# The last forward stage of a recurrent attention kernel: scaled O in the key and query space, P scaled by GpSimd, rows stored by SyncE

## The chip, the cores and the metric

The kernel runs on one core of a Trainium2 chip. The metric is the device time of one execution in microseconds (us), lower is better. Three timed runs of the kernel before gave 2970.79, 2971.32 and 2973.85 us; their median is 2971.32. A separate execution was taken with the profiler.

The engines are named as the profile names them: PE is TensorE (matmuls and transposes, with PEld for its weight loads), DVE is VectorE, ACT is ScalarE, POOL is GpSimd, SP is SyncE, which here only issues DMAs (SPq is its queue). DMAs are issued by SP and POOL, and in places by ACT. L939 is line 939 of the kernel before.

## The reference

The kernel computes the forward pass and all gradients of a conditioned transformer block, in bfloat16, for one sequence of 2048 rows of 512 values. Cut to what matters:

```
mod = silu(c) @ w_mod                      # six rows: sa, ca, ga, sb, cb, gb
h = layernorm(x) * (1 + ca) + sa
mem = mem0                                 # 8 memory rows
for s in range(64):                        # segments of 32 rows
    t = concat(mem, h[32 s : 32 s + 32])   # 40 rows
    q, k, v = t Wq, t Wk, t Wv             # 32 heads of 128
    p = softmax(mask(q k^T / sqrt(128)))
    o = (p v) Wo
    mem = o[:8];  out_s = o[8:]
x1 = x + ga * concat(out_s)
h2 = layernorm(x1) * (1 + cb) + sb
y = x1 + gb * ((sigmoid(h2 w_gate) * (h2 w_up)) w_down)
```

The outputs are y and, for a given grad_out, the gradients of x, mem0, Wq, Wk, Wv, Wo, w_gate, w_up, w_down, c and w_mod.

## The kernel before, in words

The program has four large parts that follow each other on one core: the recurrent attention forward (`phase2`, 64 stages, one per segment, up to about 950 us), the MLP forward and backward (`phase3`, 16 tiles of 128 rows, and its weight gradients), the recurrent attention backward, and the attention's weight gradients. All of the attention's intermediate results that the backward needs are kept in DRAM: V^T (`VT`), O^T (`OT`), P (`PS`), O (`OSR`), and the rows of Q and K (`QST`, `KST`).

**A forward stage.** Four heads' rows stand side by side in a 128-partition tile, three heads of 40 rows (120 columns) in a group, 11 groups in all. PE projects K, Q and V (`pass_ps`, L257 and L677), turns K and Q (L883) into the tiles `kT` and `qT` (128 partitions x 1328 columns of bf16 each), computes the scores (L893), and ACT writes their exponentials into one of two buffers ET (L895; stage s uses ET of number s mod 2). PE sums and multiplies by V (L899, L919), DVE takes the reciprocal of the sums (`rden`, L904), and the unnormalized product is evacuated, scaled by `rden`, into `Ost` by DVE (L950) and ACT (L947). PE turns `Ost` (L911, L960) into `OT`, multiplies by Wo (L223, 64 matmuls into `at_ps`), and the sum of two halves goes back to the next stage as its memory rows. `Ost` is one buffer: SP stores it to `OSR` (L1078), and the next stage may write it when that store has landed.

**P in the stages up to 62.** SP turns ET by a DMA into `Pst` (L1048); one stage later POOL scales it by `rden` in place (L1141, 120x1408 elements) and SP stores it to `PS` (L1144).

**The last stage, 63.** It does not turn by DMA. PE turns V (`turn_v`) and P (`turn_p`, L934, into PSUM tiles `pt_ps`), V^T is copied to the space of rows that are free by then, and DVE scales the turned P out of PSUM into `Pst` (L939, `scale_p`, three instructions). `Pst` is one buffer too, so L939 waits until the store of stage 62's P has landed. SP stores V^T (L1077), `Ost` (L1078), `OT` (L1081), later P (L1149) and the rows of K and Q (`late_rows`, L608 and L609). Rows of the attention's output go to the DRAM array `AOA` by `store_rows` (L347) and by `rows_b` (L811, four stores), both through POOL's queue, here as before. In the same stage POOL issues the loads of the three MLP weights (L987, L1050, L1075; 1792 KB each), into the space of Wk and Wv, and the first MLP tile's input is prepared (`first_tile_steps`).

**The first MLP tiles.** `run_pipeline` runs tiles through the steps `s0` to `s6`, deepest step first. `s0` makes the layernorm of a tile from its attention rows, x and grad_out, which `glu_load` loads through SP (L1177, L1179, L1180): DVE at L1255 to L1281, the power on POOL (L1266), the bf16 copy `xh2` on ACT (L1274; of tile 1 on POOL, L1272). `s2` multiplies by w_gate and w_up in four column chunks: for each a `gp` product (L1322) whose sigmoid ACT writes to `sg` (L1323) and an `up` product (L1326) that ACT copies to `u` (helper `evac`, L61; L63 is its DVE form). The products use a ring of five PSUM banks (`psM`). After tile 0's products PE turns w_down (L1231) through two banks (`psT`) and two of the ring, evacuated by ACT and DVE alternately; `s3` uses the result (L1353). `wT_piece` (L1220) turns w_gate and w_up in the groups after steps 2, 3 and 4 of the pipeline, each turned pair evacuated by ACT or DVE by the parity of its number plus k.

**What sets the order.** The stages' instructions keep the order in which the code writes them (`pin`); in the MLP the order of PE and ACT is written down for the first steps and a list scheduler places the rest. The tiles of the MLP (`u`, `sg`, `hh`, `h2`, ...) lie in SBUF space that the attention's pools have left; the framework adds the waits for what last used the space. Every DMA of SP's and ACT's queues raises one of eight semaphores, in turn, and every DMA of POOL's queue one of another eight.

Of the kernel before, what the change touches and what calls it, by code (L numbers as in the profile page):

```python
# [10 lines left out]
ALU = mybir.AluOpType  # L11
# [29 lines left out]
class K:  # L41
# [72 lines left out]
    def phase0(self):  # L114
        nc, tc, cfg, io = self.nc, self.tc, self.cfg, self.io
        const = self.const
        D, DC = cfg.D, cfg.DC
        self.ident = const.tile([128, 128], BF16, name="ident")
        make_identity(nc, self.ident[:])
        self.foldsel = const.tile([128, 32], BF16, name="foldsel")  # L120
        fs2 = const.tile([128, 2, 32], BF16, name="foldsel2")
        for i in range(2):
            nc.vector.tensor_tensor(fs2[:, i, :], self.ident[:, 64 * i:64 * i + 32], self.ident[:, 64 * i + 32:64 * i + 64],
                                    op=ALU.add)
        nc.vector.tensor_tensor(self.foldsel[:], fs2[:, 0, :], fs2[:, 1, :], op=ALU.add)
        self.foldhalf = fs2
        self.later = []
        self.ones = const.tile([128, 128], BF16, name="ones")
        nc.vector.memset(self.ones[:], 1.0)
        L, M = cfg.L, cfg.M  # L130
        mT32 = const.tile([120, 120], F32, name="maskT32")
        nc.gpsimd.memset(mT32[:], 0.0)
        for b in range(3):
            sl = mT32[:, b * L:(b + 1) * L]
            nc.gpsimd.affine_select(out=sl, in_=sl, pattern=[[1, L]], compare_op=ALU.is_ge, fill=NEG,
                                    base=b * L, channel_multiplier=-1)
            nc.gpsimd.memset(mT32[:, b * L:b * L + M], 0.0)
# [195 lines left out]
    def store_rows(self, psp, pool, ft, dram, name, tag, then=None):  # L333

        nc = self.nc
        tb = pool.tile([128, 128], BF16, name=name + "_tb", bufs=1 if name.endswith("_b") else 2)
        nc.vector.tensor_copy(tb[:].rearrange("p (r c) -> p c r", c=self.cfg.DC), ft[:])

        def f():
            tp = psp.tile([128, 128], BF16, name=name + "_tp", tag=tag)  # L340
            nc.tensor.transpose(tp[:], tb[:], self.ident[:])
            rb = pool.tile([128, 128], BF16, name=name + "_rb")
            nc.vector.tensor_copy(rb[:], tp[:])
            if callable(dram):
                dram(rb)
            else:
                nc.gpsimd.dma_start(dram.rearrange("r (c x) -> (r c) x", x=128), rb[:])  # L347
            if then is not None:
                then(rb)

        self.later.append(f)
# [97 lines left out]
    def phase2(self):  # L449
# [15 lines left out]
        with ExitStack() as ctx:  # L465
# [107 lines left out]
            def part3(t, pi):  # L573
                return t[:, pi * PW:min((pi + 1) * PW, G * GW)].rearrange("p (g x) -> p g x", x=GW)
# [233 lines left out]
            def rows_b(rb, b):  # L808

                for i in range(4):  # L810
                    nc.gpsimd.dma_start(self.AOA[4 * b + i + 1, 32:32 + M, :].rearrange("r (c x) -> (r c) x", x=128),  # L811
                                        rb[32 * i:32 * i + 32, :])

            tail = TailRows(self, sb2, psp, psp, 1, "ao", rows_b, (8, 16, 8), ptag="p", bufs=1)
# [35 lines left out]
            for s in range(NS):  # L850
# [55 lines left out]
                def transposes_part(src, pi, w=GW, m=128):  # L906
# [4 lines left out]
                        nc.tensor.transpose(ps[:, j, 0:m], src[0:m, g * w:g * w + GW], self.ident[0:m, 0:m])  # L911
                    return ps[:, 0:n, 0:m], n

                def pv(pi, or_ps=None):
                    or_ps = or_ps or ps_f32("or_ps")
                    n = min(PG, G - pi * PG)
                    for j in range(n):
                        g = pi * PG + j
                        nc.tensor.matmul(or_ps[:, j, :], lhsT=ET[:, g * GW:(g + 1) * GW], rhs=Vst[:, g * GW:(g + 1) * GW],  # L919
                                         start=True, stop=True)  # L920
                    return or_ps
# [12 lines left out]
                        nc.tensor.transpose(ps[:, j, :], ET[:, g * GW:(g + 1) * GW], self.ident[:, :])  # L934
                    turned_p[pi] = ps

                def scale_p(pi):
                    n = min(PG, G - pi * PG)
                    nc.vector.tensor_tensor(Pst[0:120, pi * PG:pi * PG + n, :], turned_p[pi][0:120, 0:n, :],  # L939
                                            rden[:, pi * PG:pi * PG + n].unsqueeze(2).to_broadcast([120, n, 128]), op=ALU.mult)  # L940

                def ost(pi, or_ps, eng):
                    n = min(PG, G - pi * PG)
                    if eng == "act":
                        for j in range(n):
                            g = pi * PG + j
                            nc.scalar.activation(Ost[0:120, g * GW:(g + 1) * GW], or_ps[0:120, j, :], AF.Copy,  # L947
                                                 scale=rden[:, g:g + 1])
                        return
                    nc.vector.tensor_tensor(part3(Ost, pi)[0:120, 0:n, :], or_ps[0:120, 0:n, :],  # L950
                                            rden[:, pi * PG:pi * PG + n].unsqueeze(2).to_broadcast([120, n, 128]), op=ALU.mult)

                def ott_first():
                    ps, n = transposes_part(Ost, 0, m=120)
                    self.evac("dve", part3(OT, 0)[:, 0:n, 0:120], ps)

                def ott_rest():
                    ps = psp.tile([128, 2 * PG, GW], BF16, name="tps", tag="p")
                    for g in range(PG, G):
                        nc.tensor.transpose(ps[:, g - PG, 0:120], Ost[0:120, g * GW:(g + 1) * GW], self.ident[0:120, 0:120])  # L960
                    for pi in (1, 2):
                        n = min(PG, G - pi * PG)
                        self.evac("act", part3(OT, pi)[:, 0:n, 0:120], ps[:, (pi - 1) * PG:(pi - 1) * PG + n, 0:120])
# [110 lines left out]
                if s == NS - 1:  # L1074
                    nc.gpsimd.dma_start(self.w_down, io["B_w_down"].rearrange("(fc p) d -> p fc d", p=128))  # L1075
                    for g0, t, w in ((0, RAs[0]["k"], 8), (8, RAs[0]["q"], G - 8)):
                        nc.sync.dma_start(self.VT[s, :, g0:g0 + w, :], t[:, 0:w * GW].rearrange("p (g x) -> p g x", x=GW))  # L1077
                nc.sync.dma_start(self.OSR[s], gl3(Ost))  # L1078
                at_ps = outproj()
                if s == NS - 1:  # L1080
                    nc.sync.dma_start(self.OT[s], gl3(OT))  # L1081
# [12 lines left out]
                    self.store_rows(psp, sb2, ft, self.AOA[s + 1, 0:32, :], "at", "p")  # L1094
                    self.pop_later()
                    self.pop_later()
                    turn_p(1)
                    self.pop_later()
                    for pi in (2, 0, 1):
                        scale_p(pi)  # L1100
                    break
                evac_turned()
                if s in first_tile[0]:
# [41 lines left out]

                if s < NS - 1:
                    norms.append(norm)
            self.glu_first[0] = self.glu_load(0, nc.sync)
            nc.sync.dma_start(self.PS[NS - 1], Pst[:])  # L1149
            late_rows()  # L1150
            self.pinned = self.pin(i0)

    def glu_tiles(self):
# [29 lines left out]
    def phase3(self):  # L1183
# [9 lines left out]
        with ExitStack() as ctx:  # L1193
# [32 lines left out]
            def wdT_pieces():  # L1226
                for f0 in range(0, FC, 7):
                    for c in range(DC):
# [4 lines left out]
                                  tp[:, 0:7, :].rearrange("p i f -> p (i f)"))  # L1233

            turns = {2: [wT_piece(w_gate, w_gateT, 0, 4, None)],
                     3: [wT_piece(w_gate, w_gateT, 4, 10, 0), wT_piece(w_up, w_upT, 0, 4, 1)],
                     4: [wT_piece(w_up, w_upT, 4, 10, 1)]}

            ins = {}
# [6 lines left out]
            def s0(j):  # L1246
# [21 lines left out]
                xh2 = sbp.tile([128, D], BF16, name="xh2", bufs=5)  # L1268
                xhf = sbp.tile([128, D], F32, name="xhf", tag="f32tmp", bufs=5)
                nc.vector.tensor_scalar(xhf[:], x1[:], mv[:, 0:1], rstd[:, 0:1], op0=ALU.subtract, op1=ALU.mult)  # L1270
                if j == 1:
                    nc.gpsimd.tensor_copy(xh2[:], xhf[:])  # L1272
                else:
                    nc.scalar.activation(xh2[:], xhf[:], AF.Copy)  # L1274
# [1235 lines left out]
```

## Time and profile before

| What | us |
|---|---|
| median of three runs | 2971.32 |
| the profiled execution's own time | 2972.47 |
| its span, first to last instruction | 2970.7 |
| PE busy | 2903.7 (98%) |
| DVE, ACT, POOL busy | 1624.5, 1341.6, 1237.7 |
| last stage's first K projection (L257) | starts at 930.54 |
| tile 0's first product with w_gate (L1322) | starts at 950.89 |
| tile 1's first product with w_gate | starts at 966.99 |

The page gives busy times, the chain of work that ended last, and the costliest groups; the trace also answers for stretches of time: a timeline of each engine (start, duration, engine, line, operation, and in brackets the idle time before it with what ended it), the waits summed by who waited for whom, and busy times with the granted TensorE clock in chosen windows. A DMA's row on SPq is the time in which SP issued it, not the transfer.

### The profile page before, as it was taken

How to read it: one execution, taken by the hardware profiler on the slowest of the kernel's cores; microseconds unless marked ns; L12 is line 12 of the kernel's file. 1: busy time of each engine (PE TensorE's matmuls, PEld its weight loads, DVE VectorE, ACT ScalarE, POOL GpSimd, SP SyncE). 2: the span in 40 equal slices, each digit the busy share in tenths (PEclk: the TensorE clock that was granted, in tenths of full speed). 3: DMA queues.
4: the chain of work that ended last, by engine and by line, in shares of the span. 5: the costliest groups of instructions: out<-in, count | busy, mean ns of one | idle time of the engine just before them, and what ended most of it. 6: DMA issues, size and time to landing. Idle time of an engine off the chain costs nothing.

```text
span 2970.7 us, 105319 instructions
## 1 busy us (share of the span) xinstructions
PE 2903.7 (98%) x43742; PEld 1813.8 (61%) x43816; DVE 1624.5 (55%) x3689; ACT 1341.6 (45%) x3234; POOL 1237.7 (42%) x2487
## 2 busy tenths in 40 slices
PE   6999999999999999999999999999999999999999
PEld 3666666666665544445677777777777754445545
DVE  5665566656656888733455666566666532750011
ACT  3666666666666444312355555555555520110011
POOL 2555545555555222221344444444444432772111
PEclk9999999999999999999999999999999999999999
DMA  9988888989899899998699999999999997886565
GB/s 311 228 223 217 213 214 228 217 213 225 218 227 273 221 231 229 241 290 272 187 251 253 251 252 249 253 248 244 257 253 251 250 276 245 248 265 192 162 215 172
DMA packets 838066, 703.01 MB, mean 237 GB/s; under 512 B 537698, under 2 KB 710162, under 8 KB 836692
## 3 DMA queue, kind: packets, MB, share of 16 engines
q1 hardware_dynamic: 711972, 485.29, 66.0%
q0 software_dynamic: 54512, 148.63, 16.1%
q10 hardware_dynamic: 71104, 62.34, 6.6%
q8 instruction: 345, 5.65, 0.8%
q14 instruction: 133, 1.09, 0.1%
HBM read 294.99 MB, written 276.35 MB: 192 GB/s over the span
## 4 chain that ended last, share of the span: by engine, by line
PE 90%; DMA 4%; DVE 2%; issue 1%; ACT 1%; SPq 0%; POOL 0%; DVEq 0%; POOLq 0%; ACTq 0%
PE gps L2289 14%; PE pass_ps L257 14%; PE dh_ps L215 8%; PE g_ps L1912 5%; PE pass_ps L677 5%; PE gps5o L2304 4%; PE dhq_ps L223 4%; PE at_ps L223 4%; PE mm L1393 3%; PE gps L1572 3%; PE dh_tps L215 3%; PE turn_ps L883 2%; PE mm L1368 2%; PE mm L1353 2%; PE tps L1829 2%
## 5 line engine op out<-in xcount | busy, mean ns | idle before, releaser
L2289 PE MATMUL gps<-rows,hrows 128*128 128x512 bf16 (+2 forms) x2124 | 413.6, 355 | 1.9
L2289 PEld LDWEIGHTS <-hrows 128*128 128x128 bf16 x2160 | 211.1, 98 | 204.5 <-issue 0.9
L1141 POOL TENSOR_TENSOR Pst<-Pst,rden 120x1408 bf16<-120x1408 bf16 x63 | 159.8, 2537 | 312.7 <-issue 190.0
L63 DVE CAST ot<-gps 128x512 bf16<-128x512 f32 (+3 forms) x76 | 48.2, 634 | 298.3 <-PE gps L2289 217.0
L1957 POOL COPY dOst<-RAd 96x512 bf16<-96x512 bf16 x128 | 75.4, 613 | 296.9 <-DVE RAd L63 296.7
L61 ACT ACTIVATE ot<-gps 128x512 bf16<-128x512 f32 (+3 forms) x75 | 41.2, 550 | 343.3 <-PE gps L2289 208.0
L677 PE MATMUL pass_ps<-Wv,hT 128*32 128x512 bf16 (+2 forms) x2304 | 186.6, 357 | 0.0
L2293 POOL DMA_DIRECT2D out_dram<-ot x104 | 78.8, 758 | 251.1 <-DVE ot L63 128.6
L257 PEld LDWEIGHTS <-hT 128*32 128x32 bf16 x4096 | 115.9, 97 | 98.5 <-issue 7.5
L63 DVE CAST Vst<-pass_ps 96x512 bf16<-96x512 f32 x128 | 87.3, 682 | 106.3 <-ACT RBv L61 102.8
L215 PE MATMUL dh_ps<-WvT,dVT 128*32 128x512 bf16 x2048 | 133.3, 380 | 1.7 <-DVE RBd L63 0.2
L223 PE MATMUL at_ps<-Wo,OT 128*32 128x256 bf16 x4096 | 127.6, 275 | 2.7 <-DMA Wo<-in_A_Wo_dram 1.7
L677 PE MATMUL pass_ps<-Wv,hb 128*32 128x512 bf16 (+2 forms) x636 | 126.5, 339 | 0.3 <-POOL hb L430 0.3
L257 PE MATMUL pass_ps<-Wk,hT 128*32 128x512 bf16 x2048 | 124.1, 383 | 2.1 <-POOL hT L563 1.1
L257 PE MATMUL pass_ps<-WoT,dyT 128*32 128x256 bf16 (+1 forms) x3072 | 122.6, 308 | 0.9 <-ACT dyT L2038 0.9
L257 PE MATMUL pass_ps<-Wq,hT 128*32 128x512 bf16 x2048 | 123.0, 379 | 0.3 <-DVE RBk L63 0.3
L223 PE MATMUL dhq_ps<-WqT,dQT 128*32 128x256 bf16 x4096 | 123.1, 273 | 0.1
L215 PE MATMUL dh_ps<-WkT,dKT 128*32 128x512 bf16 x2048 | 122.3, 380 | 0.0
L2304 PE MATMUL gps5o<-WoT,rows 128*128 128x512 bf16 x549 | 120.4, 379 | 0.9 <-DMA rows<-OSR 0.4
L223 PEld LDWEIGHTS <-dQT 128*32 128x32 bf16 x4096 | 109.5, 97 | 16.3 <-issue 0.4
L317 DVE TENSOR_TENSOR dST<-dh_ps,dST 128x512 bf16<-128x512 f32 x64 | 44.3, 692 | 130.4 <-ACT dST L316 130.4
L1899 DVE SCALAR_TENSOR_TENSOR dS<-dp_ps,Pst_l 128x480 bf16<-128x480 f32 (+1 forms) x192 | 106.2, 608 | 12.3 <-PE dp_ps L1897 8.0
(478 smaller groups left out, 7033.9 us busy)
## 6 DMA issues: line engine op xcount, KB each, us to landing
OSR<-Ost SPq DMA_DIRECT2D x64, 352.0 KB
OT<-OT SPq DMA_DIRECT2D x64, 352.0 KB
PS<-Pst SPq DMA_DIRECT2D x64, 352.0 KB
Pst_l<-PS SPq DMA_DIRECT2D x64, 352.0 KB
OT_l<-OT SPq DMA_DIRECT2D x64, 352.0 KB
DVR<-rows_x POOLq DMA_DIRECT2D x64, 352.0 KB, 6.3
DKR<-rows_x POOLq DMA_DIRECT2D x64, 352.0 KB, 5.7
DQR<-rows_x POOLq DMA_DIRECT2D x64, 352.0 KB, 3.3
```

The lines of the kernel that those rows point to most:

```text
L63: return nc.vector.tensor_copy(out, in_)
L215: self.nc.tensor.matmul(ps[32 * j:32 * j + 32, :], lhsT=lhsT, rhs=w, start=(n < 4), stop=(n >= total - 4), tile_position=(0, 32 * j))
L223: nc.tensor.matmul(ps[32 * j:32 * j + 32, :], lhsT=x[k], rhs=w[k][:, 256 * d:256 * d + 256], start=(n == 0), stop=(n == total - 1), tile_p ...
L257: self.nc.tensor.matmul(ps[32 * j:32 * j + 32, :], lhsT=lhs(c), rhs=rhs, start=(c == 0), stop=(c == DC - 1), tile_position=(0, 32 * j))
L677: nc.tensor.matmul(ps[32 * j:32 * j + 32, o * E:(o + n) * E], lhsT=lhsT, rhs=wc[:, 3 * a + hl:3 * (a + n - 1) + hl + 1:3, :], start=(c == ...
L1141: nc.gpsimd.tensor_tensor(Pst[0:120, :, :], Pst[0:120, :, :], rden[:, :].unsqueeze(2).to_broadcast([120, G, 128]), op=ALU.mult)
L1393: nc.tensor.matmul(hp[:], lhsT=xT[:, fc, :], rhs=wT[:, fc, :], start=(n == 0), stop=(n == 2 * FC - 1))
L1572: nc.tensor.matmul(ps[:], lhsT=h2r[:, j, c * 128:(c + 1) * 128], rhs=xr[:, j, :], start=(j == 0), stop=(j == NT - 1))
L1899: nc.vector.scalar_tensor_tensor(out=part3(dS, pi)[:, :, 0:120], in0=ps[:, 0:n, 0:120], scalar=cfg.scale, in1=part3(Pst, pi)[:, :, 0:120], ...
L1912: nc.tensor.matmul(ps[:, j, 0:w], lhsT=lh[:, g * GW:(g + 1) * GW], rhs=rh[:, g * GW:g * GW + w], start=True, stop=True)
L2289: nc.tensor.matmul(ps[:, 0:ng * E], lhsT=hrows[:, tp_, c * 128:(c + 1) * 128], rhs=rows[:, tp_, 0:ng * E], start=(tp_ == 0), stop=(tp_ == ...
L2304: nc.tensor.matmul(pss[gg][:], lhsT=rows[:, t, gg * E:(gg + 1) * E], rhs=dyrows[:, t, :], start=(n == 0), stop=(n == NTP - 1))
```

## The change

- In stage 63 the scaled product O goes to the space of `kT` (groups 0 to 7) and `qT` (groups 8 to 10) in place of `Ost`; it is turned from there, and stored to `OSR` in two DMAs.
- In stage 63 the turned P is copied by ACT, unscaled, to the other exponential buffer (ET 0), and POOL scales it there in place with one instruction. The store to `PS` reads that buffer.
- The row stores after stage 63's second half (one `store_rows`, four of `rows_b`) go through SP's queue.
- SP's order at the stage's end is P's store, the rows of K and Q, then tile 0's loads.
- In the MLP, the second group of turns swaps ACT and DVE, and `xh2` of tiles 3 and 4 is copied by POOL in place of ACT.

```diff
+        self.row_q = nc.gpsimd
...
-                nc.gpsimd.dma_start(dram.rearrange("r (c x) -> (r c) x", x=128), rb[:])
+                self.row_q.dma_start(dram.rearrange("r (c x) -> (r c) x", x=128), rb[:])
...
-                    nc.gpsimd.dma_start(self.AOA[4 * b + i + 1, 32:32 + M, :].rearrange("r (c x) -> (r c) x", x=128),
+                    self.row_q.dma_start(self.AOA[4 * b + i + 1, 32:32 + M, :].rearrange("r (c x) -> (r c) x", x=128),
...
+                def o_rows(a, b):
+                    t, o = (Ost, 0) if s < NS - 1 else (KT, 0) if b <= 2 * PG else (QT, 2 * PG)
+                    return t[:, (a - o) * GW:(b - o) * GW]
...
-                def scale_p(pi):
+                def copy_p(pi):
                     n = min(PG, G - pi * PG)
-                    nc.vector.tensor_tensor(Pst[0:120, pi * PG:pi * PG + n, :], turned_p[pi][0:120, 0:n, :],
-                                            rden[:, pi * PG:pi * PG + n].unsqueeze(2).to_broadcast([120, n, 128]), op=ALU.mult)
+                    nc.scalar.activation(part3(ETs[(s + 1) % 2], pi)[0:120, 0:n, :], turned_p[pi][0:120, 0:n, :], AF.Copy)
+
+                def scale_p():
+                    p = gl3(ETs[(s + 1) % 2])[0:120, :, :]
+                    nc.gpsimd.tensor_tensor(p, p, rden[:, :].unsqueeze(2).to_broadcast([120, G, 128]), op=ALU.mult)
...
-                            nc.scalar.activation(Ost[0:120, g * GW:(g + 1) * GW], or_ps[0:120, j, :], AF.Copy,
+                            nc.scalar.activation(o_rows(g, g + 1)[0:120, :], or_ps[0:120, j, :], AF.Copy,
...
-                nc.sync.dma_start(self.OSR[s], gl3(Ost))
+                for a, b in ((0, G),) if s < NS - 1 else ((0, 2 * PG), (2 * PG, G)):
+                    nc.sync.dma_start(self.OSR[s, :, a:b, :], o_rows(a, b).rearrange("p (g x) -> p g x", x=GW))
...
                     self.store_rows(psp, sb2, ft, self.AOA[s + 1, 0:32, :], "at", "p")
+                    self.row_q = nc.sync
                     self.pop_later()
                     self.pop_later()
                     turn_p(1)
                     self.pop_later()
                     for pi in (2, 0, 1):
-                        scale_p(pi)
+                        copy_p(pi)
+                    scale_p()
+                    self.row_q = nc.gpsimd
                     break
...
+            nc.sync.dma_start(self.PS[NS - 1], gl3(ETs[NS % 2]))
+            late_rows()
             self.glu_first[0] = self.glu_load(0, nc.sync)
-            nc.sync.dma_start(self.PS[NS - 1], Pst[:])
-            late_rows()
...
-                     3: [wT_piece(w_gate, w_gateT, 4, 10, 0), wT_piece(w_up, w_upT, 0, 4, 1)],
+                     3: [wT_piece(w_gate, w_gateT, 4, 10, 1), wT_piece(w_up, w_upT, 0, 4, 0)],
...
-                if j == 1:
+                if j in (1, 3, 4):
                     nc.gpsimd.tensor_copy(xh2[:], xhf[:])
```

The other lines of the diff replace `Ost` by `o_rows` in the DVE form of `ost`, in `ott_first` and in `ott_rest`.

More of the change, by code (lines that the diff above doesn't have):

```diff
@@ L946, in ost @@
                             g = pi * PG + j
-                            nc.scalar.activation(Ost[0:120, g * GW:(g + 1) * GW], or_ps[0:120, j, :], AF.Copy,
+                            nc.scalar.activation(o_rows(g, g + 1)[0:120, :], or_ps[0:120, j, :], AF.Copy,
                                                  scale=rden[:, g:g + 1])
                         return
-                    nc.vector.tensor_tensor(part3(Ost, pi)[0:120, 0:n, :], or_ps[0:120, 0:n, :],
+                    o = o_rows(pi * PG, pi * PG + n).rearrange("p (g x) -> p g x", x=GW)
+                    nc.vector.tensor_tensor(o[0:120, :, :], or_ps[0:120, 0:n, :],
                                             rden[:, pi * PG:pi * PG + n].unsqueeze(2).to_broadcast([120, n, 128]), op=ALU.mult)
                 def ott_first():
-                    ps, n = transposes_part(Ost, 0, m=120)
-                    self.evac("dve", part3(OT, 0)[:, 0:n, 0:120], ps)
+                    ps = ps_b16("tps")
+                    for g in range(PG):
+                        nc.tensor.transpose(ps[:, g, 0:120], o_rows(g, g + 1)[0:120, :], self.ident[0:120, 0:120])
+                    self.evac("dve", part3(OT, 0)[:, 0:PG, 0:120], ps[:, 0:PG, 0:120])
                 def ott_rest():
@@ L959, in ott_rest @@
                     for g in range(PG, G):
-                        nc.tensor.transpose(ps[:, g - PG, 0:120], Ost[0:120, g * GW:(g + 1) * GW], self.ident[0:120, 0:120])
+                        nc.tensor.transpose(ps[:, g - PG, 0:120], o_rows(g, g + 1)[0:120, :], self.ident[0:120, 0:120])
                     for pi in (1, 2):
```

## The prediction

> **What bounds the kernel now.** I read the page first. TensorE is busy 98% of the span and the chain of work that ended last is PE for 90%, so only a gap in PE, or one that the change opens there, moves the time. The edits lie between the last forward stage and the first MLP tiles, so next came PE's timeline of that stretch (start, duration, idle time and releaser in brackets).
>
> ```profile
> 940.18 0.33 PE L934 MATMUL pt_ps<-ident,ET 128*128 128x128 bf16 x3
> 942.44 0.38 PE L911 MATMUL tps<-ident,Ost 120*128 120x120 bf16 x4 [1.93 <-DVE Ost L950]
> ...
> 943.69 3.13 PE L223 MATMUL at_ps<-Wo,OT 128*32 128x256 bf16 x64
> ...
> 955.42 0.92 PE L1322 MATMUL mm<-Wk,Wq 128*128 128x448 bf16 x4
> ...
> 961.19 0.55 PE L1231 MATMUL tp<-ident,Wv 128*128 128x128 bf16 x7 [1.91 <-DVE w_downT L63]
> ```
>
> PE has two gaps here, 1.93 and 1.91 us. The first waits for Ost, which DVE may write only when the previous stage's store of it has landed. The second waits for a DVE evacuation, late because DVE first waited 1.46 us for the store of P (L939) and then spent 1.75 us scaling P. Each gap is under 0.1% of the time.
>
> The windows view by microsecond (busy time with counts, then granted clock, DMA share, GB/s) shows that the first gap costs more than itself:
>
> ```profile
> 941.00:942.00 1.00, 0.00 (x0) 0.00 (x0) 0.31 (x1) 0.33 (x2) 0.00 (x0) 1.00 1.01 389
> ...
> 943.00:944.00 1.00, 1.00 (x14) 0.58 (x16) 0.90 (x5) 0.32 (x1) 0.00 (x0) 0.50 1.04 355
> 944.00:945.00 1.00, 1.00 (x28) 0.72 (x24) 0.96 (x2) 0.98 (x3) 0.74 (x2) 0.50 1.05 396
> 945.00:946.00 1.00, 1.00 (x24) 0.73 (x20) 0.29 (x1) 0.99 (x2) 1.00 (x2) 0.50 0.94 376
> ```
>
> The clock is 0.50 for three microseconds, and L223's 64 matmuls take 3.13 us, against 1.94 at 927.00 one stage earlier: 1.2 us. The DMA engines are full, at 355 to 434 GB/s from 937 to 958. So I read SyncE's own timeline and its waits last (waits: us in total, times, longest).
>
> ```profile
> 945.31 0.40 SPq L1078 DMA_DIRECT2D OSR<-Ost  x1
> 945.81 0.45 SPq L1081 DMA_DIRECT2D OT<-OT  x1
> ...
> 956.49 0.34 SPq L1149 DMA_DIRECT2D PS<-Pst  x1
> 958.31 0.32 SPq L608 DMA_DIRECT2D KST<-RA1k  x1
> ```
>
> ```profile
> SPq L608 <- DMA OSR<-Ost: 1.5, 1, 1.5
> SPq L1149 <- DMA VT<-RA0q: 1.3, 1, 1.3
> ```
>
> SyncE's DMAs use eight semaphores in turn, and each waits until the one eight places before it has landed. The store of P goes out at 956.49 because VT<-RA0q has just landed, not because P is late (DVE ended it at 954.49). The store behind it goes out at 958.31, when OSR<-Ost lands.
>
> **The change, part by part.**
>
> *O in K^T's and Q^T's space.* The same DVE and ACT instructions with other targets, and one more store on SyncE. The 1.93 us gap shrinks to what the stage before shows (0.38 before L911 at 925.95) and its slow clock goes: up to 1.5 + 1.2 us. I count nothing of it, since the next part stops PE later, at a point that DMA sets.
>
> *P copied by ScalarE, scaled by GpSimd.* DVE loses its wait and 1.75 us. ACT gains three copies of bf16 PSUM, 1.4 us by the row OT<-tps (0.47 each for 480 columns), in a place where it idled 1.73 us (before L1323 at 951.89). POOL gains one 120x1408 product, 2.53 us by L1141, and loses five DMA issues, 0.63 + 2.00 us. All hidden. If ACT's cover were gone it would cost at most the 1.4.
>
> *What the copy collides with.* The exponential buffer ET0 lies at bytes 161600 to 164416 of a partition, and the first MLP tile's u at 161376 to 164960, in both built programs. Before, u waited only for old readers of that space, and ACT wrote it at 952.60. In the changed program this u (ACT, L61) waits for GpSimd's product and for the landing of the store of P, which now reads ET0. Behind u on ACT stand all further sg and u evacuations. PE's product ring has five banks: the seventh product, L1322 at 955.42, needs the bank that u frees, and behind it stand the w_down transposes.
>
> *When that store lands.* GpSimd is done by about 954.4 (copies end by 951.8, + 2.5). SyncE is later. Five row stores and the split O store now stand before it, so its partner eight places back is the 1024-column part of O. That is 256 of the 352 KB that landed at 958.3; the DMA before it, VT<-RA0q, landed at 956.4 (the trace's semaphore records); so 957.9. None of those DMAs is issued earlier than now, since each waits for an older landing. The old store of P took 4.4 us from its issue at 956.49 to 960.9, behind five loads (256 KB) that now come after it. KST<-RA1k, 192 KB, took 3.0 from 958.31. Bounds: 2.5 (QST<-RA1q, issued 959.76) to 8.8 (the store of P of the stage before, 943.94 to 952.7, under full load). I take 3.0: landing at 960.9, close to the light-load row, since the weight loads end at 957.1.
>
> *The cost on PE.* u from 961.0 to 961.55, seventh product at 961.6 instead of 955.42: **+6.2 us**. Of this the second gap is paid back, **-1.9**: DVE has nothing left of P to scale, and its h and db are ready by 959.3, before the transposes run at 963. ACT then has five evacuations queued, 0.42 apart (its L61 and L1323 rows at 973.20 to 974.05), beside 1.5 us of products and the first transposes: hidden.
>
> *The clock.* A wait of at least 6.2 us will slow the clock if 1.93 did; the 1.91 us gap left it at 1.00. Bounds 0 to 2.4 (two such dips); I take one at its measured price, **+1.2**.
>
> The Trainium skill (TensorE: Matmul & The Clock Gate, "What's actually happening") lets the clock fall after an idle window of about 3.4 us and rise after a busy one, with windows that run free. The trace's dip lasted one such window but followed a gap of only 1.93 us, so here the measurement decides. By that rule, as an estimate, PE is slow for 3.4 to 6.8 us after the wait; half of it, 1.7 to 3.4, would stand for my 1.2, and the sum would be +5.6 to +7.3.
>
> *Row stores through SyncE.* Nothing in the MLP reads these rows soon. The loads of tile 0 (for its late steps) and tile 2 come behind them: tile 2's would be issued by about 965 instead of 960.7 to 963.1 and land some 3.5 us later, before DVE wants them at 968.86 + 4. Zero; each us beyond that would show on DVE.
>
> *Turns and xh2.* The swap of evacuating engines at L1220 moves one 1024-column copy from DVE (0.69) to ACT (1.02). Following the new order through the two-bank ring, the last product of that group ends within 0.1 us of now: zero. xh2 of tiles 3 and 4 goes from ACT (0.63) to POOL (1.13, L1272). In tile 3's group PE waited 1.15 for ACT (L1220 at 992.27), then DVE's copy binds (L1220 at 992.93): 0.66 is won, less 0.3 because DVE's L1278 took 0.98 instead of 0.69 beside POOL's cast: **-0.4**. Bounds 0 and -0.7. Tile 4 has no PE gap.
>
> Sum: +6.2 - 1.9 + 1.2 - 0.4 = **+5.1 us**. The profiled execution took 2972.47 (span 2970.7 and 1.8 around it), which gives 2977.6; the median shown is 2971.32, 1.15 lower, so I forecast **2976.4**. Later phases are PE-bound and carry the delay to the end.
>
> **The rivals.** A measurement can tell about 0.2%, 5.9 us, from no change.
>
> 1. *Hidden:* the store lands before ACT comes to u, or u's wait is short. Then the second gap and the 0.4 are won and the first gap is lost again to the loads: w_up lands near 951 (a row store behind it on POOL's queue, issued at 944.26, took 6.7) and w_down at 957.1 (PE's weight load waited 0.5 us for it). -2.3: 2969.0. For: P is scaled 3 us before its store goes out. Against: SyncE's waits of 1.3 and 1.5 us at just this place. 0.12.
> 2. *The store lands late (slower):* same mechanism, but it takes the old store's 4.4 us: 962.3, +1.4, 2977.8; with the 8.8 of full load, 2982.2. It is slower by over 0.2% once the landing passes 961.75, since each us there is one of PE. For: the nearest row of that very tensor. Against: five loads fewer ahead. 0.20.
> 3. *Two clock dips:* the wait ends late in a window, so a second one follows at half clock: +1.2, 2977.6. For: nothing in the trace but the dip itself. Against: only one dip there, ended by PE's work. 0.08. (The page named above would make this the more usual outcome.)
> 4. *It does not free O:* if the 1.93 us wait stayed, the time would be as forecast, because the later wait swallows it. No chance of its own.
>
> **How the numbers follow.** The forecast's own case has 0.60 and spans 2973 to 2977.2 (landing 959.5 to 961.7, dip 0 to 1.2). Its weight and most of the hidden case are within 0.2%: 0.70. Cases 2 and 3 are slower: 0.28. Faster by over 0.2% needs 5.9 us, more than both gaps; 0.02. The range 2971.5 to 2980 leaves out the hidden case and the far end of case 2.
>
> **What would show it.** Right: ACT's first u starts near 961 behind a wait for the store of P; PE idles 6 us or more before L1322's seventh product, then runs below full clock; the gap at w_downT is gone; P's store is issued near 957.9 although GpSimd ended before 955. Wrong: u near 952, P's store issued when GpSimd ends, PE waiting for w_up or w_down instead, or a DVE wait for tile 2's rows.

## The result and the profile after

The changed kernel's median of 14 runs is 2980.34 us (2972.03 to 2986.08), that of the kernel before in the same comparison 2972.86 (2968.01 to 2981.98, 14 runs). The ratio is 1.0022 (95% interval 1.0013 to 1.0030), some 6.5 us slower. The median lies 0.3 above the top of the range that was forecast (2971.5 to 2980); by the ratio, from the 2971.32 shown before, it is 2977.9, inside the range. The 0.22% lies just above the 0.2% that was taken there as the line between no change and slower. Executions of one kernel scatter by several us, so the steps are read from the profiles, of which there is one for each kernel. The profiled execution took 2976.83 us (span 2975.0), 4.4 more than the one before.

PE's timeline of the changed kernel, the same stretch as in the prediction (L1337 is the product with w_gate, L1341 that with w_up, L1246 the turns of w_down):

```profile
940.32 1.93 PE L224 MATMUL at_ps<-Wo,OT 128*32 128x256 bf16 x64
...
949.60 0.93 PE L1341 MATMUL mm<-Wk,Wq 128*128 128x448 bf16 x4 [1.56 <-DMA Wk<-in_B_w_up_dram]
...
959.36 1.65 PE L1337 MATMUL mm<-Wk,Wq 128*128 128x448 bf16 x4 [5.80 <-ACT u L61]
960.80 1.70 PE L1341 MATMUL mm<-Wk,Wq 128*128 128x448 bf16 x4
962.30 1.19 PE L1246 MATMUL tp<-ident,Wv 128*128 128x128 bf16 x14
```

Both old gaps are gone and the 64 matmuls run at full clock. In their place PE waits 1.56 us for w_up and 5.80 for u, and the two products behind that take 1.44 and 1.50 from start to start instead of 0.76. ACT, POOL and SyncE in turn:

```profile
958.76 0.54 ACT L61 ACTIVATE u<-mm 128x448 bf16<-128x448 f32 x1 [10.09 <-DMA PS<-ET]
```

```profile
947.85 2.74 POOL L948 TENSOR_TENSOR ET<-ET,rden 120x1408 bf16<-120x1408 bf16 x1 [1.19 <-ACT ET L944]
```

```profile
956.02 0.34 SPq L1163 DMA_DIRECT2D PS<-ET  x1
...
968.71 2.94 SPq L1361 DMA_TRANSPOSE hhT<-hh  x1
```

GpSimd is done at 950.59. SyncE issues the store 5.4 later, when its partner has landed (the DMA eight places before it, OSR<-kT, by the semaphore records at 956.0). The store lands at 958.7 and u starts. The windows view (length of the window, busy time with counts of PE, PEld, DVE, ACT, POOL, then granted clock, DMA share, GB/s) shows the clock halved from 956.0 to 962.8, two windows, the first inside the wait:

```profile
954.00:955.00 1.00, 0.00 (x0) 0.00 (x0) 0.30 (x1) 0.00 (x0) 0.77 (x1) 1.00 0.81 302
...
956.00:957.00 1.00, 0.00 (x0) 0.00 (x0) 0.95 (x2) 0.00 (x0) 0.00 (x0) 0.50 0.29 101
...
961.00:962.00 1.00, 1.00 (x5) 0.38 (x3) 0.00 (x0) 0.59 (x2) 0.00 (x0) 0.50 0.32 92
```

Profiles differ in when stage 63 comes, so from here times are counted from the start of stage 62's 64 matmuls with Wo (927.00 before, 925.48 after); "first" and "seventh" are tile 0's products, "tile 1" and "tile 2" the first product of that tile. hhT is hh of tile 0, turned by a DMA of SyncE's; PE's product at L1383 reads it.

| kernel | first | seventh | tile 1 | tile 2 | ratio to before (95%) |
|---|---|---|---|---|---|
| before | 23.89 | 28.42 | 39.99 | 56.36 | 1 |
| changed | 21.65 | 33.88 | 44.86 | 61.42 | 1.0022 (1.0013 to 1.0030) |
| E1 P in Ost | 23.35 | 30.79 | 40.15 | 61.50 | 0.9996 (0.9976 to 1.0017) |
| E2 rows by POOL | 22.53 | 35.78 | 47.65 | 64.21 | 1.0005 (0.9984 to 1.0027) |
| E3 store by POOL | 21.65 | 33.53 | 43.20 | 59.76 | 1.0009 (0.9988 to 1.0030) |
| E4 warm wait | 21.92 | 35.59 | 45.27 | 61.82 | 1.0002 (0.9980 to 1.0023) |
| E5 P in Ost, hhT first | 21.83 | 29.52 | 38.88 | 55.44 | 1.0000 (0.9990 to 1.0009) |
| E6 before, rows by SyncE | 26.54 | 31.08 | 43.53 | 63.56 | 1.0021 (1.0009 to 1.0033) |
| E7 before, only O | 22.43 | 30.06 | 40.53 | 56.90 | 1.0011 (1.0002 to 1.0019) |
| E8 before, only turns | 24.89 | 29.43 | 39.84 | 56.40 | 1.0014 (1.0002 to 1.0026) |
| E9 hhT first | 21.66 | 32.99 | 43.80 | 60.35 | 1.0010 (0.9997 to 1.0023) |
| E10 store later | 25.34 | 37.90 | 48.91 | 65.46 | 1.0040 (1.0027 to 1.0053) |
| E11 as E5, old turns | 21.65 | 28.17 | 38.42 | 54.80 | 0.9994 (0.9983 to 1.0005) |
| E12 as E1, old turns | 21.92 | 27.66 | 38.91 | 57.18 | 1.0005 (0.9995 to 1.0015) |

Part of the spread in "first" arises ahead of the edits: in E1, E2, E6, E7 and E10 PE waited 0.69 to 2.90 us in stage 63 for DVE's reciprocal (L905); in E6 DVE in its turn waited 2.34 for a result of POOL. The other profiles have no such wait above 0.2. Differences between columns of one row are safer than those between rows.

### The profile page after: what moved, and what is told of

Same layout as the page of the kernel before. It is cut to its first block, busy times and chain, and to the rows that moved or that the text cites. A ratio compares the mean times of both kernels' runs of the same rounds, so it can differ in the third digit from the quotient of the medians.

```text
span 2975.0 us, 105398 instructions
## 1 busy us (share of the span) xinstructions
PE 2916.0 (98%) x43816; PEld 1818.1 (61%) x43816; DVE 1626.8 (55%) x3685; ACT 1342.0 (45%) x3236; POOL 1235.5 (42%) x2485
## 4 chain that ended last, share of the span: by engine, by line
PE 90%; DMA 3%; DVE 2%; issue 1%; ACT 1%; SPq 0%; POOL 0%; DVEq 0%; POOLq 0%; ACTq 0%
PE gps L2304 14%; PE pass_ps L258 14%; PE dh_ps L216 8%; PE g_ps L1927 5%; PE pass_ps L678 5%; PE gps5o L2319 4%; PE dhq_ps L224 4%; PE at_ps L224 4%; PE mm L1408 3%; PE gps L1587 3%; PE dh_tps L216 3%; PE turn_ps L884 2%; PE mm L1368 2%; PE mm L1383 2%; PE tps L1844 1%; PE mm L1337 1%
```

## The experiments

Theory: the first u must wait for the landing of the store of P, since it lies over ET 0. Rival: the delay comes from something else that the change added (GpSimd's product, ACT's copies, SyncE's longer queue). E1 to E5 and E9 to E12 start from the changed kernel, E6 to E8 from the one before.

**E1, P in Ost.** The copy, the product and the store use the buffer that O left:

```diff
-  nc.scalar.activation(part3(ETs[(s + 1) % 2], pi)[0:120, 0:n, :], ...)
+  nc.scalar.activation(part3(Ost, pi)[0:120, 0:n, :], ...)
...
-  nc.sync.dma_start(self.PS[NS - 1], gl3(ETs[NS % 2]))
+  nc.sync.dma_start(self.PS[NS - 1], gl3(Ost))
```

> Changed kernel, with one thing different: the copy of P, GpSimd's product and the store of P use Ost, which the last stage no longer writes, in place of the exponential buffer ET 0. Same instructions, same queues, same order; only the space under the first MLP tile's u is no longer read by the store of P. Theory (u waits for the landing of the store of P because it lies over ET 0): ACT's first u starts near 950.5 instead of 958.76, PE's seventh product near 953.5 instead of 959.36, the half clock at 956 to 963 is gone, PE then waits about 1 us for w_down, and tile 1's first product starts near 964 instead of 970.34; time 6 to 7 us below the changed kernel, 1 to 2 below the one before. Rival (the delay comes from GpSimd's product, the copies on ACT or SyncE's longer queue): all of these are still here, so u stays near 958 and the time stays at the changed kernel's.

Measured: u starts at 955.54 behind its own product, no longer behind a store, and tile 1's first product comes at 40.15 instead of 44.86. But tile 2's comes at 61.50, no earlier than in the changed kernel. PE's and SyncE's timelines of E1:

```profile
979.09 0.61 PE L1383 MATMUL mm<-Wv,hhT 128*128 128x512 bf16 x1 [3.15 <-DMA hhT<-hh]
```

```profile
972.48 3.50 SPq L1361 DMA_TRANSPOSE hhT<-hh  x1
```

PE now waits 3.15 us for hhT, and that wait halves the clock for two windows more: from tile 1 to tile 2 it takes 21.35 instead of 16.56. hh itself is ready (DVE ended it at 965.96); SyncE issues hhT's DMA at 972.48, behind 22 others issued one after the other from 960.73. The theory of u holds, and a second wait was hidden behind the first, which neither the theory nor the rival had.

**E2, the rows by POOL again.**

```diff
   self.store_rows(psp, sb2, ft, self.AOA[s + 1, 0:32, :], "at", "p")
-  self.row_q = nc.sync
```

> Changed kernel, with the five row stores of the last stage's second half issued by POOL again; everything else as changed, P still in ET 0. Theory: the store of P moves five places forward in SyncE's ring of eight semaphores, its partner landed long ago, so SyncE issues it when GpSimd's product ends, near 951 instead of 956.0. It then transfers beside the two stores of O, that of O^T and the load of w_down: landing between 954 (3.0 after issue) and 957 (6 after issue). PE's seventh product follows the landing by 0.7: 954.7 to 957.7 instead of 959.36, so 1.7 to 4.7 us are won against the changed kernel, and up to 1.5 more if the clock doesn't dip. Rival (the row stores are neutral, as the prediction priced them by themselves, and the store lands late because of the traffic): landing still near 958.7, no gain.

Measured: 2.8 us worse at tile 2 by the profile, while the timed runs can't tell it from the changed kernel. POOL's timeline:

```profile
954.00 2.06 POOL L812 DMA_DIRECT2D AOA<-ao_b_rb  x4
956.08 2.55 POOL L948 TENSOR_TENSOR ET<-ET,rden 120x1408 bf16<-120x1408 bf16 x1
```

The row stores now stand ahead of the product on POOL, which ends at 958.63; SyncE issues the store at 958.65, and the last of its 16 parts lands at 965.6, 7.0 later. The expected gain of 1.7 to 4.7 didn't come: moving the row stores moved the product as well, and an earlier place among SyncE's eight semaphores was worth nothing. Issued at 28.0 instead of 30.5, on the same queue, the store landed at 35.0 instead of 33.2; the windows view has the DMA engines' share at 1.01 to 1.08 from 957 to 963.

**E3, the store of P by POOL.**

```diff
   scale_p()
+  nc.gpsimd.dma_start(self.PS[s], gl3(ETs[(s + 1) % 2]))
...
-  nc.sync.dma_start(self.PS[NS - 1], gl3(ETs[NS % 2]))
```

> Changed kernel, with only the store of P moved from SyncE's queue to POOL's, straight behind the product that scales it; the row stores stay with SyncE, P stays in ET 0. Theory: issued near 951, landing 954 to 957, seventh product 0.7 later, so again 1.7 to 4.7 us less than the changed kernel and up to 1.5 more if the clock doesn't dip. Rival (the wait is for GpSimd's product or ACT's copies): they are unchanged, and the first u should stay near 958.7.

Measured, POOL's and ACT's timelines:

```profile
955.15 0.63 POOL L1115 DMA_DIRECT2D PS<-ET  x1 [0.30 <-POOL ET L948]
```

```profile
962.67 0.54 ACT L61 ACTIVATE u<-mm 128x448 bf16<-128x448 f32 x1 [9.74 <-DMA PS<-ET]
```

The store is issued 5.1 us earlier (25.4 instead of 30.5) and takes 7.4 instead of 2.6 to land, so u starts only 0.35 earlier (32.93 against 33.28). By the semaphore records it lands behind w_down (960.7) and the store of rows that follow it in POOL's queue (961.4), at 962.5, and the windows view has the DMA engines' share at 1.03 to 1.06 from 955 to 959. So SyncE's order is not all that holds the landing: without it the store lands 0.4 earlier. Whether the traffic as a whole or the place behind w_down in POOL's own queue holds it here, this run can't tell; E2, on SyncE's queue, points to the traffic. The Trainium skill (DMA: Bandwidth & Descriptors, "Issuing engines are not separate DMA queues") says that another issuing engine saves only the time of issuing; this run agrees, with 0.4 us won by an issue 5.1 earlier. Most of the 1.66 us won at tile 1 is clock: the slow window fell elsewhere (955.1, behind a wait of 2.46 for w_up), and the way from the seventh product to tile 1 took 9.67 instead of 10.98.

**E4, a warm wait.** 28 products of 128x448 into an unused bank ahead of the seventh product.

```diff
+  if j == 0 and ch == 3:
+      for i in range(28):
+          nc.tensor.matmul(acc_ps[:, 0:CH], lhsT=hdT[:, 0, :], rhs=w_gate[:, 0, 0:CH], start=True, stop=True)
   gp = mm()
```

> Changed kernel, with 28 products of 128x448 added on PE just before the seventh product of the first MLP tile; their result goes to a bank that nobody reads before it is overwritten, so they add work and change no output. About 28 x 0.19 = 5.3 us of work in a wait of 5.8. Theory of the clock term: the clock stays at 1.00 from 953 to 963, the last two products take 0.76 each from start to start instead of 1.44 and 1.50, and tile 1's first product starts about 1.5 us earlier than 970.34; the wait itself stays (u near 958.8). If the clock plays no part, tile 1's first product stays at 970.3; if the added work overruns the wait, it comes later.

Measured, PE's timeline:

```profile
956.60 5.46 PE L1337 MATMUL acc_ps<-Wk,Wq 128*128 128x448 bf16 x28
964.29 0.92 PE L1340 MATMUL mm<-Wk,Wq 128*128 128x448 bf16 x4 [2.23 <-ACT u L61]
965.04 0.92 PE L1344 MATMUL mm<-Wk,Wq 128*128 128x448 bf16 x4
```

The clock stays at 1.00 and the last two products take 0.76 each. From the seventh product to tile 1 it takes 9.68 instead of 10.98, so the slow clock cost 1.30. In this execution the store landed 1.7 later, which took the gain back.

**E6, only the row stores by SyncE, on the kernel before** (`row_q` as in the change, nothing else). After E1 this was the test of SyncE's queue by itself.

```diff
   self.store_rows(psp, sb2, ft, self.AOA[s + 1, 0:32, :], "at", "p")
+  self.row_q = nc.sync
...
   for pi in (2, 0, 1):
       scale_p(pi)
+  self.row_q = nc.gpsimd
```

> The kernel before, with only one edit of the change: the five row stores of stage 63's second half go through SyncE's queue instead of POOL's. P, O and the turns stay as before. The prediction gave this edit nothing. Theory (SyncE's queue bounds hhT): counted from stage 62's matmuls with Wo, hhT is issued at 41.5 to 43.8 instead of 39.5, lands at 47 to 49.5 instead of 45.2, and PE, which wants it at 46.93, waits 0.5 to 3 us: the time grows by as much. The prediction's price: hhT still lands before 46.9 and nothing moves.

Measured: slower by 0.21% (0.09 to 0.33). PE's and SyncE's timelines:

```profile
980.68 0.97 PE L1371 MATMUL mm<-Wv,hhT 128*128 128x512 bf16 x2 [2.90 <-DMA hhT<-hh]
```

```profile
973.79 3.11 SPq L1349 DMA_TRANSPOSE hhT<-hh  x1
```

In the kernel before, SyncE and PE (no wait):

```profile
966.54 2.71 SPq L1346 DMA_TRANSPOSE hhT<-hh  x1
```

```profile
973.93 0.38 PE L1368 MATMUL mm<-Wv,hhT 128*128 128x512 bf16 x1
```

hhT's DMA is issued at 46.7 instead of 39.5 (the kernel before: 966.54) and PE waits 2.90 for it. From tile 1 to tile 2 it takes 20.03 instead of 16.37, 3.7 more (the wait and a slow window behind it). Some of this execution's lateness lies ahead of the edit ("first" at 26.54), so by the profile only the 3.7 can be put down to SyncE's queue.

**E5, P in Ost and hhT first.** As E1, and on SyncE tile 0's five loads go behind hhT's DMA, and the written order holds for two more steps, so that six loads of later tiles no longer slip in front (with None, `glu_load` names the tiles and loads nothing):

```diff
-  self.glu_first[0] = self.glu_load(0, nc.sync)
+  self.glu_first[0] = self.glu_load(0, None)
...
   nc.sync.dma_start(hhT[:], st["hh"][:], transpose=True)
+  if j == 0:
+      self.glu_load(0, nc.sync)
...
-  if it == 4:
+  if it == 6:
       self.pin(i0, [ET.SP])
```

> Times here are counted from the start of stage 62's 64 matmuls with Wo (927.00 before, 925.48 in the changed kernel, 928.67 in the run with P in Ost). That run won the wait of u and then lost it again: PE waited 3.15 and 3.4 us for hhT, whose DMA SyncE issued at 43.8 (39.5 before), behind 22 DMAs in a row. This kernel is that one with the five loads of tile 0's late inputs put behind hhT's DMA on SyncE, and with SyncE kept in program order for two more pipeline steps, so that six loads of later tiles no longer slip in front of it. Theory (SyncE's queue is the second bound): eleven DMAs at some 0.45 less, hhT issued at 38 to 39.5, landed by 45, no wait of PE for it, tile 2's first product at 55 to 57 (before 56.36, changed 61.42, P in Ost 61.50); time 4 to 6 us below the changed kernel, level with the one before or up to 2 below. Rival (hhT is late because hh is, since hh now lies over the space that the store of P reads): hh on DVE still starts near 36 and hhT can't be issued before its partner lands, PE's waits stay above 2 us.

Measured: hhT is issued at 37.3 and landed at 41.9; PE wants it at 45.8. No wait is left there, and tile 2's first product comes at 55.44, 6.0 us ahead of the changed kernel and 0.9 ahead of the kernel before. SyncE's timeline:

```profile
958.78 0.34 SPq L1163 DMA_DIRECT2D PS<-Ost  x1
...
965.12 1.85 SPq L1363 DMA_TRANSPOSE hhT<-hh  x1
```

**E9, hhT first alone**: E5's diff without E1's, P left in ET 0.

> The changed kernel, with P left in ET 0 and only SyncE's order mended: tile 0's late inputs behind hhT's DMA, and SyncE in program order for two more pipeline steps. The fourth cell of a square: the wait of u mended or not, SyncE's order mended or not. Counted from stage 62's matmuls with Wo, tile 2's first product came at 61.42 (neither), 61.50 (only u), 55.44 (both), 56.36 in the kernel before. Theory (two waits that cover each other, and only the later one is paid): hhT now lands near 47 instead of 48.5, which PE wants at 51.8 anyway, since u still waits until 33; tile 2's first product stays at 61 to 62 and the time within 1 us of the changed kernel's. Rival (SyncE's order alone was the cost, as the run with only the row stores moved might suggest): tile 2's first product at 55 to 57.

Measured: tile 2's first product at 60.35. hhT lands at 46.8, and PE, held up by u as before, comes to it at 50.8:

```profile
960.23 0.54 ACT L61 ACTIVATE u<-mm 128x448 bf16<-128x448 f32 x1 [9.19 <-DMA PS<-ET]
```

So the square is: neither mended 61.42, only u 61.50 (57.18 in E12), only SyncE's order 60.35, both 55.44. By the profiles the two waits cover each other, and PE pays for the later one. The timed runs set only the last cell clearly apart from the first (0.9990 to 1.0009 against 1.0013 to 1.0030); the intervals of E1, E9 and E12 overlap with that of the changed kernel.

**E10, the store of P behind the rows of K and Q.**

```diff
-  nc.sync.dma_start(self.PS[NS - 1], gl3(ETs[NS % 2]))
   late_rows()
+  nc.sync.dma_start(self.PS[NS - 1], gl3(ETs[NS % 2]))
```

> The changed kernel, with the store of P put behind the four stores of the rows of K and Q on SyncE, instead of ahead of them. Counted from stage 62's matmuls with Wo. Theory (each us by which that store lands later is one of PE): issued near 32.8 instead of 30.5, behind 352 KB of rows, landing at 35.5 to 37 instead of 33.2; u and the seventh product as much later, tile 1's first product at 47 to 49 instead of 44.86, the time 2 to 4 us up. Rival (the wait is set by something else that lands at the same time, such as the store of O): landing later changes nothing, seventh product at 33.9.

Measured: the store is issued at 34.2 and u starts at 37.3, 4.0 later than in the changed kernel; so do the seventh product (37.90) and tile 2 (65.46). Of the 4.0, 0.8 is that SyncE came to this place later, 2.8 the four stores ahead, and 0.4 a longer way to landing (3.1 instead of 2.6). Each us by which the store lands later is one of PE:

```profile
965.77 0.54 ACT L61 ACTIVATE u<-mm 128x448 bf16<-128x448 f32 x1 [10.42 <-DMA PS<-ET]
```

**E7, only O, and E8, only the turns and xh2**, on the kernel before. E7 has the change's `o_rows` and the split store:

```diff
-  nc.sync.dma_start(self.OSR[s], gl3(Ost))
+  for a, b in ((0, G),) if s < NS - 1 else ((0, 2 * PG), (2 * PG, G)):
+      nc.sync.dma_start(self.OSR[s, :, a:b, :], o_rows(a, b).rearrange("p (g x) -> p g x", x=GW))
```

E8 has the last two pieces of the change's diff (`turns` and `xh2`) and one edit more that the change does not have: the same condition in `s1` changed too, so that PE turns h and db of tiles 3 and 4, in place of two DMAs of SyncE's:

```diff
-                if j == 1:
+                if j in (1, 3, 4):
                     tp = tp8()
```

> The kernel before, with only the part on O: scaled O in the space of K^T and Q^T in the last stage, stored in two DMAs. P, the row stores and the turns stay as before. Counted from stage 62's matmuls with Wo. Theory (the first gap is no gain by itself, because later waits take it): the 1.93 us wait for Ost and the slow clock behind it go, the 64 matmuls of stage 63 start at 14.9 instead of 16.7 and take 1.94 instead of 3.13, tile 0's first product starts at 21.7 instead of 23.9; then PE waits 1.5 us or more for w_up and the gap at w_downT grows, so tile 1's first product comes at 39.5 to 40 (39.99 before) and the time stays within 0.5 us. Rival (the gap was on the path): tile 1's first product comes 2 to 2.7 earlier, and so does the end.

Measured for E7: the gap of 1.93 and the slow matmuls are gone ("first" 1.46 earlier), then PE waits for w_up and pays the slow clock there instead, and for w_downT once more (1.01); tile 1 comes 0.5 later than before:

```profile
953.84 1.60 PE L1336 MATMUL mm<-Wk,Wq 128*128 128x448 bf16 x4 [1.23 <-DMA Wk<-in_B_w_up_dram]
```

By itself the part on O gains nothing, as the theory had it; the timed runs even have it 0.11% slower (0.02 to 0.19).

> The kernel before, with only the edits in the MLP: ACT and DVE swapped in the second group of turns, xh2 of tiles 3 and 4 copied by POOL. The prediction gave 0 and -0.4. From the first product of tile 1 to that of tile 2 it was 16.37 before and 16.55 to 16.56 in four profiles with these edits; from tile 2 to tile 3, 21.87 before and 21.95 to 21.98. Theory: the edits cost +0.18 and +0.09 by themselves and show the same here. Rival (the prediction's terms, hidden in the changed kernel by its later position): 16.37 and 21.5.

Measured for E8: from tile 1 to tile 2 it takes 16.56, the +0.19 of the other profiles. From there on the edit in `s1` shows. PE waits for DVE's h, which only the turning of tile 3 by PE wants so early, and again for tile 4 (1.34):

```profile
995.34 0.40 PE L1295 MATMUL tp<-ident,h 128*128 128x128 bf16 x4 [1.35 <-DVE h L1278]
```

From tile 2 to tile 3 it takes 23.10, and from tile 3 to tile 4 20.98 instead of the 18.80 of the other profiles. So E8's time, 0.14% up, is not the price of the change's edits. For tile 3, E5 and E11 stand: 21.95 with the edits, 21.85 without.

**E11, both mended and the old turns** (E5), and **E12, P in Ost and the old turns** (E1), both with

```diff
-  3: [wT_piece(w_gate, w_gateT, 4, 10, 1), wT_piece(w_up, w_upT, 0, 4, 0)],
+  3: [wT_piece(w_gate, w_gateT, 4, 10, 0), wT_piece(w_up, w_upT, 0, 4, 1)],
...
-  if j in (1, 3, 4):
+  if j == 1:
```

> P in Ost and hhT first on SyncE, as in the run that had both, and the turns and xh2 of the MLP as before: what the experiments point to as the best of the parts. Counted from stage 62's matmuls with Wo: tile 2's first product at 55.3 to 56 (16.37 behind tile 1's instead of 16.56), tile 3's 21.87 behind that instead of 21.95, so 0.3 less than the 77.39 of the run with both, and 1 us less than the 78.23 of the kernel before. By the time that is 0 to 0.05% below the kernel before, which a measurement of five rounds can't tell from no change. If the turns are no cost, tile 3's first product is at 77.4 again.

Measured for E11: tile 2 at 54.80, tile 3 at 76.65 (78.23 before, 83.38 changed). Its time is 0.9994 of the kernel before (0.9983 to 1.0005): faster than the changed kernel, whose interval doesn't touch it, and not to be told from the one before.

> The run with P in Ost came out at 0.9996 of the kernel before by its timed runs (0.9976 to 1.0017), although its one profile shows PE waiting 3.15 us for hhT and tile 2's first product no earlier than in the changed kernel. This is that kernel again with the turns and xh2 as before, so that it differs from the best of the parts in SyncE's order alone. Counted from stage 62's matmuls with Wo. Theory (SyncE's queue is the second bound, also in other executions): hhT is issued at 43 to 44.5, lands at 48 to 50.5, PE wants it at 45 to 47 and waits 2 to 4 us; from the first product of tile 1 to that of tile 2 it takes 18.5 to 21.5 instead of 16.38. Rival (that wait was an accident of one execution): hhT lands before PE wants it, 16.4 from tile to tile, and tile 2's first product at 55 to 56.

Measured for E12: hhT issued at 43.2, landed at 48.6, wanted at 46.0; from tile 1 to tile 2 it takes 18.27 instead of 16.38. The second wait shows in another execution too. PE's timeline:

```profile
979.17 0.60 PE L1383 MATMUL mm<-Wv,hhT 128*128 128x512 bf16 x2 [2.69 <-DMA hhT<-hh]
```

## Why the prediction was right, and where it was not

- **The wait of u (+6.2):** the seventh product came 5.46 later (33.88 against 28.42). The store landed 2.6 after its issue instead of 3.0, and the issue at 30.54 stood against 30.9. E1 shows the cause by taking it away, E10 by lengthening it.
- **Why the store lands then:** the prediction named SyncE's partner as what holds the issue. That is what held the issue, but E3 and E2 show that freeing it frees next to nothing: issued 5.1 and 2.5 earlier, the store landed 0.4 earlier and 1.9 later. It also had that no older DMA would be issued earlier than before; in this execution O's store went out at 17.42 instead of 18.31, and landed at 30.48.
- **The second gap (-1.9):** gone, 1.89 (from the seventh product to tile 1, 11.57 before and 9.68 with the clock kept up).
- **The clock (+1.2):** 1.30 by E4. Two windows came, as in the third rival, but one of them lay inside the wait and cost nothing.
- **Turns and xh2 (0 and -0.4):** +0.19 and +0.09. E5 against E11 shows both prices (16.56 and 16.38, 21.95 and 21.85). The swap gives ACT a fourth copy of 1.02 in a two-bank ring; that this makes the 0.19 is argued, not shown. At tile 3, PE was to win the 0.66 us between ACT's copy and DVE's; but the transposes behind wait for DVE's copy whatever ACT does, and that copy came 0.29 later, since h before it ran beside POOL's cast (0.98 instead of 0.69, as forecast), so there was nothing to win:

```profile
994.50 0.98 DVE L1293 TENSOR_TENSOR h<-h2a,Wv 128x512 bf16<-128x512 f32 x1
```

```profile
996.74 0.61 PE L1235 MATMUL tp<-ident,Wk 128*128 128x128 bf16 x8 [1.25 <-DVE Wq L63]
```

- **The sum (+5.1):** 5.15 at tile 3's first product (83.38 against 78.23). That it fits so closely is luck in part: u's wait was put 0.7 too high, and the turns and xh2 were put 0.7 too low. The forecast of 2976.4 stands 0.4 from the profiled execution, luck again, since that execution reached stage 62's matmuls 1.5 earlier than the one before (925.48 against 927.00). The median of the runs is 4 higher; the interval of the ratio, 3.9 to 8.9 us, takes in the 5.15. Two readings in the working are off without bearing on the sum: the forecast's own case goes down to 2973.8 by its own bounds, not 2973, and the store of P under full load took 8.7, not 8.8.
- **The row stores (0):** the step that was wrong though the sum was not. It looked for who reads the rows and for the loads behind them, and did not ask for hhT, which stands behind those loads in the same queue. In the changed kernel hhT lands at 48.5 and PE, late by u, wants it at 51.8: hidden. E6 prices the edit by itself at 0.21%, as much as the whole change loses; it does not add to the price of u, since the two waits cover each other.
- **The first rival (hidden, 2969.0):** its price was wrong for the same reason. With u's wait gone (E12) the time is 1.0005 of the kernel before, not 0.9992; hhT takes over. That holds by the profiles of E1 and E12, while the timed runs of E1 and E12 alone could not tell it from no change. By the profiles, only with both waits gone does the time come near that rival (E11, profiled at 2971.74).
- **The first gap, worth nothing:** right, and E7 shows it without u's wait: w_up and w_downT take it.

What stays open: how much of the 6.5 us of the timed runs is u in each execution and how much hhT; one profile of each kernel can't tell.

## What to carry to other kernels

When a step is moved to another queue, list everything that stands behind it in that queue down to the first transfer that the busiest engine waits for, not only the readers of what was moved. When a buffer is reused, ask what the next phase lays over it and which landing that then waits for. And where two waits cover each other, mending one may show nothing in the time: test both together before calling a cause harmless.

## What the runs showed of the hardware

- The slow clock came in windows of 3.41 us (3.41, 6.83 or 10.24 in all), and whether a gap brought one was not a matter of its length alone: gaps of 1.04 (E1), 1.23 (E7) and 2.46 us (E3) did, gaps of 1.56 (changed), 1.81 (E11) and 2.69 us (E12) did not. The Trainium skill (TensorE: Matmul & The Clock Gate, "What's actually happening") has windows of that length that run free, with which the lengths agree; it has the clock fall after an idle window, and here much shorter gaps were enough.
- The same 352 KB took 2.6 us from issue to landing on SyncE in the changed kernel, where the DMA engines' share had fallen to 0.29 at the issue, 7.0 in E2, where it stayed above 1 for four microseconds more, and 7.4 on POOL in E3.
- Beside POOL's product of 120x1408, DVE's addition of 128x512 took 2.91 us instead of 0.69 and ended 0.55 behind the product (951.14 and 950.59 in the changed kernel, 956.03 and 955.48 in E1), as if it had waited for it. DVE's h beside POOL's cast, 0.98 instead of 0.69, ended 0.54 behind the cast (995.48 and 994.94). POOL's product took 2.74 there and 2.55 in E2, where DVE stood idle. The 2.2 us of DVE cost nothing here, since DVE's h of the same tile then waits for the landing of O's store. That wait came with the change as well (the kernel before has none), and it is hidden, since PE turns h only at 965.71:

```profile
948.23 2.91 DVE L1272 TENSOR_TENSOR x<-t,Wk 128x512 f32<-128x512 f32 x1
...
956.05 0.69 DVE L1293 TENSOR_TENSOR h<-h2a,Wv 128x512 bf16<-128x512 f32 x1 [1.75 <-DMA OSR<-kT]
```
